# Moving 640 columns of the first w1 load behind phi, onto DMA engines 0 to 4

## The chip, the cores and the metric

One core of one Trainium2 chip. The metric is the device time of one execution in microseconds (us), on the core that runs it; lower is better.

## The reference, cut to what matters

Sliding-window attention over 8 batches and 8 heads, then a soft mixture of experts over the 4608 tokens:

```python
x = attention(q, k, v).reshape(4608, 512)
logits = x @ phi                       # 32 slots, 4 for each of 8 experts
d = softmax(logits, axis=0); slot_input = d.T @ x
h = maximum(slot_input[e] @ w1[e], 0)  # w1: 8 x 512 x 1024, float32
slot_out[e] = h @ w2[e]                # w2: 8 x 1024 x 512, float32
out = softmax(logits, axis=1) @ slot_out
```

All of w1 and w2 (33.5 MB as float32) is needed once, and only when attention is done. So the weights stream in beside the attention, and the output goes out at the end.

## The kernel before: the parts that matter

The program is a list of operations with reads and writes; a small scheduler in the file orders them for each engine and derives the waits. Two kinds of loads compete. GpSimd issues the software transfers (queue q0), which cast float32 to bf16 on the way: all of q, k, v, w2 and nearly all of w1. SyncE issues the hardware transfers (queue q1), which in this kernel don't cast. One of those is the first thing of the kernel: the first 2048 of the 4096 columns of expert 0's w1, as float32, into space that a w2 load fills much later; ScalarE casts it.

```python
op(SP, lambda: spq.dma_start(
    af(w2off(0), [[1, 2048]]),
    w1_rows(0)[:, :2048]), .1, -200.0,
   kind="dma", nbytes=1 << 20, sem=sem("s_w1f"), writes=b_w2[0], name="w1f")
for x in range(2):
    op(ACT, lambda x=x: act.activation(
        a(o_w1 + 1024 * x, [[1, 1024]]), af(w2off(0) + 2048 * x, [[1, 1024]]), ACTF.Copy),
        1.1, -200.0, reads=b_w2[0], writes=[b_w1[0]], name=f"w1c{x}")
# ... (cut)
def load_phi(first):          # SyncE, after the first transpose of VectorE, about 11.8 us
    op(SP, lambda: spq.dma_start(f(o_phst, [[64, 2], [1, 64]]),
        moe_phi.rearrange("(hf p two) s -> p hf (two s)", hf=2, two=2)), .1, 20.0,
       kind="dma", nbytes=65536, sem=sem("s_phi"), writes=[b_phst], name="phi", after=[first])
```

The order on q0 is: the first batch's k, q, v (six loads), the rest of expert 0's w1, the second batch's loads, and so on, and last of all small slices of w2, after whose landing only 1.3 us of work stand ahead of the next output evictions (ScalarE and VectorE copying finished results to where the stores take them from).

The softmax here doesn't subtract the row's maximum and nothing guards it: scores larger than these inputs give would overflow.

## Time and profile before

| | before |
|---|---|
| time, median | 176.98 us (176.91 to 177.19, 6 runs) |
| span of the profiled run | 175.2 us |
| first packet of q0 | 4.77 us |
| first load of k, completions of its sixteen engines | 6.49 to 7.02 us |
| last weight transfer, completions of its sixteen engines | 148.69 to 151.54 us |

The prediction shows the slices, the queues and the chain of waits. The timeline of the first 6 us (start, duration, engine, line, operation, what ended the idle time) shows the head: SyncE issues the w1 load at 0.74, GpSimd its first k load at 1.23, and ScalarE waits 3.65 us for the w1 rows.

```profile
0.74 0.37 SPq L408 DMA_DIRECT2D ar<-in_moe_w_dram  x1
...
1.23 0.67 POOL L343 DMA_DIRECT2D ar<-in_k_dram  x1 [0.79 <-POOLq L1041]
...
5.67 2.00 ACT L413 ACTIVATE ar<-ar 128x1024 bf16<-128x1024 f32 x2 [3.65 <-DMA ar<-in_moe_w_dram]
```

And the table of stretches (busy time of each engine, then granted clock, DMA share, GB/s) shows the hand-over from q1 to q0: the w1 load moves 434 GB/s between 4 and 5 us, then q0's bf16 writes count half of what they read.

```profile
3.00:4.00 1.00, 0.00 (x0) 0.00 (x0) 0.87 (x1) 0.00 (x0) 1.00 (x3) 1.00 0.82 344
4.00:5.00 1.00, 0.00 (x0) 0.00 (x0) 1.00 (x6) 0.00 (x0) 1.00 (x3) 1.00 1.08 434
5.00:6.00 1.00, 0.00 (x0) 0.00 (x0) 0.56 (x3) 0.33 (x1) 1.00 (x5) 1.00 1.06 200
```

### The profile page before, as it was taken

The page shows a single profiled execution, that of the slowest core. Times are in us where ns is not written, and L with a number is a line of the kernel's source. Part 1 is how long each engine was busy: PE and PEld are TensorE (multiplying, and loading weights), DVE is VectorE, ACT ScalarE, POOL GpSimd, SP SyncE. Part 2 cuts the span into 40 slices and gives each one's busy share as a digit, 9 for nine tenths or more (in the row PEclk, how much of TensorE's full clock was granted, in tenths as well). Part 3 has the DMA queues.
Part 4 walks back from the last instruction along what each step waited for, and adds up shares of the span by engine and source line. Part 5 has one row for each costly group of instructions (what it writes and reads, how often), then busy time and mean ns, then how long its engine had stood idle before and what let it go on. Part 6 is the DMA issues. An engine that isn't in the chain of part 4 may idle for free.

```text
span 175.2 us, 4785 instructions
## 1 busy us (share of the span) xinstructions
PE 127.4 (73%) x2102; PEld 86.0 (49%) x2102; DVE 120.7 (69%) x220; ACT 105.1 (60%) x165; POOL 44.5 (25%) x90
## 2 busy tenths in 40 slices
PE   0008667969998998998988997999776766898000
PEld 0005535746766866776756766776343323442000
DVE  6899497978998998998698798349430002699300
ACT  2404763797978969969868968965603001599000
POOL 7659502406234053027200014940000000000000
PEclk9999995699999999999999999999999999999655
DMA  6999999999999999999999999999999999999997
GB/s 191 228 210 217 211 214 208 219 210 213 216 211 214 217 213 207 218 211 217 213 209 216 217 213 221 215 219 211 209 223 215 210 192 189 270 343 418 449 423 299
DMA packets 14388, 41.26 MB, mean 236 GB/s; under 512 B 1696, under 2 KB 7328, under 8 KB 12064
## 3 DMA queue, kind: packets, MB, share of 16 engines
q0 software_dynamic: 10512, 30.41, 88.3%
q1 hardware_dynamic: 3856, 10.55, 15.7%
q8 instruction: 16, 0.26, 0.5%
q14 instruction: 4, 0.03, 0.0%
HBM read 61.93 MB, written 9.44 MB: 407 GB/s over the span
## 4 chain that ended last, share of the span: by engine, by line
DMA 33%; DVE 24%; PE 22%; ACT 7%; POOL 5%; issue 3%; POOLq 0%; DVEq 0%
DMA ar<-in_moe_w_dram 21%; DMA ar<-in_v_dram 12%; PE ps L529 6%; DVE ar L497 6%; DVE ar L945 6%; ACT ar L568 4%; POOL ar L381 3%; DVE ar L503 3%; PE ps L590 2%; PE ps L713 2%; PE ps L536 2%; DVE ar L634 2%; PE ps L623 2%; PE ps L546 2%; DVE ar L454 2%
## 5 line engine op out<-in xcount | busy, mean ns | idle before, releaser
L568 ACT ACTIVATE ar<-ps 128x1152 bf16<-128x1152 f32 (+1 forms) x32 | 37.9, 1186 | 21.5 <-PE ps L553 10.9
L529 PE MATMUL ps<-ar 128*128 128x320 bf16 (+1 forms) x128 | 23.2, 306 | 16.1 <-DVE ar L503 13.8
L497 DVE STREAM_TRANSPOSE ar<-ar 128x576 uint32<-128x576 uint32 x28 | 32.8, 1237 | 0.6 <-DMA ar<-in_v_dram 0.6
L634 DVE TENSOR_TENSOR ar<-ps,fs 96x768 bf16<-96x768 f32 (+1 forms) x32 | 26.3, 822 | 1.1
L596 ACT ACTIVATE ar<-ps 128x768 bf16<-128x768 bf16 x32 | 24.8, 809 | 3.6 <-PE ps L590 3.1
L529 PEld LDWEIGHTS ps<-ar 128*128 128x128 bf16 x128 | 10.8, 100 | 20.9 <-POOL ar L427 13.7
L623 PE MATMUL ps<-ar 128*128 128x65 bf16 x320 | 15.2, 195 | 3.4 <-ACT ar L568 2.1
L590 PE MATMUL ps<-ar 128*128 128x128 bf16 x192 | 15.8, 229 | 2.4 <-DVE ar L634 2.1
L503 DVE STREAM_TRANSPOSE ar<-ar 128x576 uint32<-128x576 uint32 x12 | 14.6, 1241 | 1.8 <-DMA ar<-in_q_dram 1.8
L623 PEld LDWEIGHTS ps<-ar 128*128 128x128 bf16 x320 | 12.1, 98 | 6.7 <-ACT ar L568 2.9
L345 POOL DMA_DIRECT2D ar<-in_k_dram x14 | 7.5, 541 | 30.5 <-DVE ar L497 15.6
L942 ACT ACTIVATE ar<-ps,fs 128x512 f32<-128x512 f32 (+1 forms) x23 | 11.4, 636 | 5.7 <-PE ps L934 5.7
L590 PEld LDWEIGHTS ps<-ar 128*128 128x128 bf16 x192 | 12.7, 118 | 3.7 <-DVE ar L634 2.3
L630 DVE RECIPROCAL fs<-ps 96x12 f32<-96x12 f32 (+1 forms) x32 | 6.5, 203 | 10.9 <-PE ps L623 10.6
L885 PE MATMUL ps<-ar 128*32 128x512 bf16 (+1 forms) x76 | 10.8, 347 | 4.3 <-DMA ar<-in_moe_w_dram 3.3
L945 DVE TENSOR_SCALAR ar<-ps,fs 128x512 f32<-128x512 f32 (+1 forms) x23 | 12.7, 627 | 1.0 <-PE ps L934 1.0
L934 PE MATMUL ps<-ar 128*128 128x512 bf16 (+1 forms) x46 | 10.2, 346 | 1.1 <-DVE ar L909 1.0
L343 POOL DMA_DIRECT2D ar<-in_q_dram x16 | 8.8, 549 | 6.1 <-DVE ar L509 6.1
L713 PE MATMUL ps<-ar 128*128 128x288 bf16 x64 | 9.8, 299 | 0.7 <-ACT ar L697 0.7
L693 ACT ACTIVATE ar<-ps 128x1024 bf16<-128x1024 bf16 x8 | 8.2, 1030 | 3.3 <-PE ps L680 3.3
L690 ACT ACTIVATE ar<-ps 128x576 bf16<-128x576 bf16 x16 | 9.5, 648 | 1.1 <-PE ps L674 0.8
L509 DVE STREAM_TRANSPOSE ar<-ar 128x160 uint32<-128x160 uint32 (+1 forms) x32 | 9.6, 413 | 0.0
(78 smaller groups left out, 190.2 us busy)
## 6 DMA issues: line engine op xcount, KB each, us to landing
ar<-in_moe_w_dram POOLq DMA_DIRECT2D x13, 1024.0 KB, 26.6
ar<-in_k_dram POOLq DMA_DIRECT2D x16, 288.0 KB, 14.5
ar<-in_q_dram POOLq DMA_DIRECT2D x16, 288.0 KB, 16.2
ar<-in_v_dram POOLq DMA_DIRECT2D x16, 288.0 KB, 15.2
out_dram<-ar SPq DMA_DIRECT2D x2, 2048.0 KB, 10.1
out_dram<-ar SPq DMA_DIRECT2D x10, 256.0 KB, 3.1
out_dram<-ar SPq DMA_DIRECT2D x2, 1024.0 KB, 6.1
ar<-in_moe_w_dram SPq DMA_DIRECT2D x1, 1024.0 KB, 4.9
```

What stands on the lines that cost most here:

```text
L497: return dve.transpose(au(o_kqv[kq] + 2304 * j + 36 * x, [[1, 18], [36, 16], [576, 2]]), au(src + 64 * 18 * x, [[32, 18], [1, 32]]))
L503: return dve.transpose(au(dst, [[1, 18], [18, 32]]), au(src, [[32, 18], [1, 32]]))
L529: pe.matmul(pf(h, 0, [[1, W]]), a(o_id, [[1, 128]]), a(msk, [[1, W]]), start=True, stop=False)
L568: eo = op(ACT, lambda P=P, W=W: act.activation(a(P, [[W, 4], [1, W]]), AP(ps, 0, [[4096, 128], [512, 4], [1, W]]), ACTF.Exp, scale=SCALE), ...
L590: last = pe.transpose(pb(bank.idx, bb * 256 + par * 32, [[64, 4], [1, 32]]), src, a(o_id, [[1, 128]]))
L596: op(ACT, lambda t=t, bank=bank: act.activation(a(o_vb[vs] + 3 * t * VBK, [[66, 12], [2, 32], [1, 2]]), pb(bank.idx, 0, [[64, 12], [1, 32] ...
L623: last = pe.matmul(pf(bank.idx + x, 65 * t, [[1, 65]]), w, a(VB + t * VBK + 66 * h, [[1, 65]]), start=True, stop=True)
L634: op(DVE, lambda hp=hp, bank=bank: dve.tensor_tensor(a(ox + 128 * hp, [[64, 2], [256, NT], [1, 64]], 0, rows), pf(bank.idx, 0, [[512, 2], ...
L713: last = pe.matmul(pf(bank.idx, 0, [[1, 288]]), a(o_phis + 128 * c, [[1, 128]]), a(o_xt[xt] + 576 * c + 288 * g, [[1, 288]]), start=(c == ...
L885: last = pe.matmul(pf(sobank[x].idx, 0, [[1, n]], 32 * j, 32), a(o_htz + 1024 * g + 128 * c + 32 * j, [[1, 32]]), a(w2off(e) + DM * c + co ...
L942: op(ACT, lambda: act.activation(dst, src(), ACTF.Copy, scale=sca), actt(cw, .1), prio + .1, reads=[bank, b_rinv], writes=wr, name=f"OE{G} ...
L945: op(DVE, lambda: dve.tensor_scalar(dst, src(), sca, None, op0=AluOp.mult), dvet(cw, True) + .08, prio + .1, reads=[bank, b_rinv], writes= ...
```

## The change

The intent: some DMA engines finish their share of the loads 2.4 us before the others. The first load is shortened for all sixteen, and what is taken away is given to engines 0 to 4 alone, later. ScalarE casts the first 1408 columns, GpSimd the other 640.

```diff
-    op(SP, ... w1_rows(0)[:, :2048] ... name="w1f")
-    for x in range(2):
-        op(ACT, ... 1024 columns ...)
+    WX = 1408
+    def w1_first(n, c0, c1, p0, pn, **kw):
+        op(SP, lambda: spq.dma_start(af(w2off(0) + 2 * c0, [[1, c1 - c0]], p0, pn),
+                                     w1_rows(0)[p0:p0 + pn, c0:c1]), .1, ...)
+    def w1_cast(n, c0, c1, prio):
+        ... op(POOL if n else ACT, lambda: pool.tensor_copy(dst, src) if n else act.activation(dst, src, ACTF.Copy), ...)
+    w1_first(0, 0, WX, 0, 128, prio=-200.0)
+    w1_cast(0, 0, WX, -200.0)
+    def w1_rest(first):
+        w1_first(1, WX, 2048, 0, 125, prio=21.0, after=[first], lag=8.0)
+        w1_first(2, WX, 2048, 125, 3, prio=22.0, after=[first], lag=8.0)
+        w1_cast(1, WX, 2048, 30.0)
...
             load_phi(first_t[0])
+            w1_rest(first_t[0])
```

(Waits and buffers of the helper are cut.)

More of the change, by code (lines that the diff above doesn't have):

```diff
@@ L405, in load_w @@
                    writes=list(wr) + rd + ([x for y in b_kqv[0] for x in y] if name[:2] == "w2" and e in (3, 4) else []))
-    op(SP, lambda: spq.dma_start(
-        af(w2off(0), [[1, 2048]]),
-        w1_rows(0)[:, :2048]), .1, -200.0,
-       kind="dma", nbytes=1 << 20, sem=sem("s_w1f"), writes=b_w2[0], name="w1f")
-    for x in range(2):
-        op(ACT, lambda x=x: act.activation(
-            a(o_w1 + 1024 * x, [[1, 1024]]), af(w2off(0) + 2048 * x, [[1, 1024]]), ACTF.Copy),
-            1.1, -200.0, reads=b_w2[0], writes=[b_w1[0]], name=f"w1c{x}")
+    WX = 1408
+    b_w1f = [Buf("w1fa"), Buf("w1fb")]
+    def w1_first(n, c0, c1, p0, pn, **kw):
+        op(SP, lambda: spq.dma_start(af(w2off(0) + 2 * c0, [[1, c1 - c0]], p0, pn),
+                                     w1_rows(0)[p0:p0 + pn, c0:c1]), .1,
+           kind="dma", nbytes=1024 if n else 1 << 20, sem=sem(f"s_w1f{n}"), writes=[b_w1f[n > 0]] + b_w2[0],
+           name=f"w1f{n}", **kw)
+    def w1_cast(n, c0, c1, prio):
+        dst, src = a(o_w1 + c0, [[1, c1 - c0]]), af(w2off(0) + 2 * c0, [[1, c1 - c0]])
+        o = op(POOL if n else ACT, lambda: pool.tensor_copy(dst, src) if n else act.activation(dst, src, ACTF.Copy),
+            actt(c1 - c0), prio, reads=[b_w1f[n]], writes=[b_w1[0]], name=f"w1c{n}")
+        for x in b_w2[0]:
+            x.r.append(o)
+    w1_first(0, 0, WX, 0, 128, prio=-200.0)
[4 more added lines that the diff above has]
+        w1_cast(1, WX, 2048, 30.0)
     def const_ops():
```

## The prediction

> **What bounds the kernel now.** I read three views in this order. First the page's forty slices and its queue table. A slice is 4.38 us of the 175.2 us span.
>
> ```profile
> DVE  6899497978998998998698798349430002699300
> ...
> DMA  6999999999999999999999999999999999999997
> GB/s 191 228 210 217 211 214 208 219 210 213 216 211 214 217 213 207 218 211 217 213 209 216 217 213 221 215 219 211 209 223 215 210 192 189 270 343 418 449 423 299
> ...
> q0 software_dynamic: 10512, 30.41, 88.3%
> q1 hardware_dynamic: 3856, 10.55, 15.7%
> q8 instruction: 16, 0.26, 0.5%
> ```
>
> The DMA row has a nine in every slice but the first and the last. The loads run on q0, are cast from float32 to bf16 on the way, and fill the engines' time until about 151 us; then q1 stores the output until the end. No compute engine is near that: VectorE is the busiest of them in the first two thirds and idles after it.
>
> Second, the chain of waits that ended last, from 108 us on.
>
> ```profile
> 109.37 4.05 POOL ar L381 x6
> ...
> 115.33 36.21 DMA ar<-in_moe_w_dram
> 151.54 0.04 issue
> 151.58 0.30 PE ps L885
> 151.88 0.02 issue
> 151.90 0.44 DVE ar L909
> 152.34 0.05 issue
> 152.39 0.42 PE ps L934 x2
> 152.81 0.03 issue
> 152.84 8.63 DVE ar L945 x15
> ```
>
> The last weight transfer is issued at 115.33 us and lands at 151.54 us. Its 36.21 us are queueing, since it is only 64 KB: GpSimd issues far ahead of the transfers, so a delay of a few us in an issue costs nothing. From the landing it is about 1.3 us to the next evictions, and then 21 us of stores. The kernel therefore ends when **the slowest of the sixteen DMA engines** has moved its share.
>
> Third, the engines are not equally late. The page can't show that, but the trace keeps, for each transfer, the sixteen moments at which its semaphore is counted up, one for each engine. For the last weight transfer seven engines finish at 148.69 to 149.21 us, one at 149.77, and eight at 151.05 to 151.54. For the first load of k all sixteen lie between 6.49 and 7.02 us. So eight engines fall 2.4 us behind on the way. The sixteen instruction fetches on q8 account for it: 0.5% of sixteen engines' 175.2 us is 14 us, or 0.9 us for each fetch of 16 KB, and two of them on each of eight engines give the lag, with some waiting. The table of stretches agrees: the engines' share falls just when seven of them are out of loads and the stores have not begun.
>
> ```profile
> 148.00:149.00 1.00, 0.71 (x7) 0.71 (x8) 0.49 (x2) 0.37 (x1) 0.00 (x0) 1.00 1.23 163
> 149.00:150.00 1.00, 0.97 (x10) 0.63 (x7) 1.00 (x4) 1.00 (x4) 0.00 (x0) 1.00 0.77 103
> 150.00:151.00 1.00, 0.93 (x8) 0.42 (x6) 0.79 (x3) 0.56 (x2) 0.00 (x0) 1.00 1.14 241
> ```
>
> The last two columns are the share of the DMA engines (above 1 where packets overlap) and the GB/s: 0.77 and 103 between 149 and 150 us.
>
> **What the Trainium skill says.** "DMA: Bandwidth & Descriptors", section "Why a DMA increments its semaphore by 16 and not by 1", says that a transfer runs on the largest number of engines up to 16 that divides its slowest dimension, and that hardware transfers take the lowest-numbered ones. 125 partitions give 5 engines, 25 rows each, and 3 partitions give 3 engines, one row each. That is the point of the odd split. Every hardware transfer of the kernel before uses all sixteen, so its trace neither confirms nor denies this. Section "Queues, rings and completion order" says that an engine goes round-robin between queues, switching at whole packets. The trace fits it at the start: q0's first packet starts at 4.768 us, 6 ns after the first engine has finished its share of the first w1 load, and not before. Section "Latency and other measured facts" puts the first byte of a software transfer at about 1 us. GpSimd's first load is issued at 1.23 us and takes 0.67 us, so by that it is ready near 2.9 us (an estimate from that page) and has been waiting behind w1; no record shows when it was ready. "GPSIMD Engine Reference", section 4.1, says that one-input elementwise work on GpSimd is roughly at line rate; no such cast is in the trace before.
>
> **The change part by part.**
>
> Taken from the start: the first w1 load shrinks from 2048 to 1408 float32 columns, so its rows from 8192 to 5632 bytes, eight rows to an engine. The trace has 309 ns for an undisturbed 8192-byte packet of that load and 22 ns for a 256-byte packet of phi. A straight line through the two is 13 ns plus 0.036 ns a byte: 217 ns for 5632 bytes and 105 ns for 2560 bytes (estimates). Each engine saves 8 x (309 - 217) = 0.74 us, and q0 starts at about 4.0 us in place of 4.77, if it is ready by then, which the 2.9 us above says it is.
>
> Added behind phi, from about 12 us on: 25 x 105 = 2.63 us on engines 0 to 4, and one row more, 2.73 us, on engines 0 to 2. Net, **engines 5 to 15 have 0.74 us less to do, engines 3 and 4 have 1.89 us more, engines 0 to 2 have 1.99 us more.** The bytes read from memory stay the same.
>
> At the end of the loads: the late eight engines, if none of 0 to 4 is among them, finish at 150.3 to 150.8 us. The early ones that got the extra rows finish at 148.7 to 149.2 plus 2.0, which is 150.7 to 151.2. So the last landing moves from 151.54 to between 150.8 and 151.2, **0.35 to 0.74 us earlier**. The extra of 2 us nearly fills the lag of 2.4 us, which looks like a size chosen for it.
>
> ScalarE's two casts of 1024 columns (1.05 us each, at 5.67 us) become one of 1408, some 1.4 us. ScalarE then idles until 15.53 us: nothing gained. GpSimd gets one cast of 640 columns, which I put at 0.5 to 1 us; GpSimd is 25% busy, and its issues lead the landings by 14 to 26 us (median of the issue table), so nothing lost. SyncE's two issues at 0.38 us each lie beside other work. Earlier landings of the first q, k and v load buy nothing directly: VectorE is at its memsets until 10.57 us and k had landed at 7.02.
>
> From the last landing everything follows at the same distance: the late engines save 0.74 us of their own work, and the chain of PE, VectorE and store follows the landing. Sum: 177.02 - 0.5 = **176.5 us**.
>
> **The rivals.**
>
> One: **engines 0 to 4 are among the late eight.** The records carry no engine numbers, so the trace before can't exclude it. Then their last landing goes from 151.5 to 153.5 and the time to about 179. Against it speaks that the size fits the lag of the other engines so well; I give it one chance in eight.
>
> Two: **q0 is not ready at 4.0 us.** Then the start leaves a hole in place of a gain, the late engines end where they did, and engines 0 to 2 end at 148.7 to 149.2 plus 2.7, up to 151.9: between no change and 0.3 us slower, so 177.0 to 177.3. The fit of the first-byte figure speaks against it.
>
> Three: **GpSimd's queue stalls.** Its cast stands in program order among the load issues, and waits for rows that alternate with q0's packets (362 ns for 4608 bytes): up to 26 x (105 + 362) = 12 us after phi's first packet at 15.54, so until 27.7 us. Loads behind it would be issued late. The 14 us or more that an issue leads its landing cover that, except where the next batch's q, k, v land late and VectorE waits. Its wait for loads of v is only 0.6 us in all now, and batch 1's two k loads land at 18.3 and 19.7 us for a use at 23.23: 3.5 us of slack against at most 2 us of delay. The end would hardly see it.
>
> Four: **the time is hidden by the stores.** Engines out of step at 151 us have come into step at 155.3 to 155.7 us for the sixth store (the same completion records), because it waits for evictions. If evictions rather than the engines set the pace there, only the landing of the last weights counts, and the gain is the lower figure, 0.35 us. That stays within the range.
>
> **Range and chances.** The main line gives 176.3 to 176.7, rivals two and four 176.7 to 177.3, run to run spread is 0.3 us. An 8 in 10 range of 175.9 to 177.4 leaves out rival one. Two per cent is 3.5 us. More than the 0.74 us cannot be saved, so faster by over 2% is nearly excluded (0.01). Even rival one gives only 1%, so slower by over 2% needs it together with a stall (0.03).
>
> **What would show it.** Right: q0's first packets near 4.0 us; new q1 packets of 2560 bytes, 128 of them, near 105 ns; the sixteen completions of the last weight transfer within about 1 us, the last at 150.8 to 151.2; a higher share of the DMA engines between 149 and 150 us; the chain of waits still through the last weight transfer. Wrong: a first q0 packet still at 4.77 (rival two); a last landing after 152 us with a few engines alone at the end (rival one); a long wait of GpSimd's new cast followed by VectorE waiting for loads (rival three).

## The result, and the profile after

The changed kernel takes 177.61 us (177.53 to 177.77, 6 runs) against 176.98. The ratio is 1.0034 with a 95% interval of 1.0022 to 1.0047: within 2%, but clearly slower, where 0.5 us faster was predicted. Ratios here are the mean time of one kernel's fast runs over that of the other's of the same rounds, so not quite the ratio of the quoted medians.

The page of the changed kernel, slices and queues:

```profile
DMA  6999999999999999999999999999999999999997
GB/s 169 194 212 232 227 216 215 216 214 207 221 213 208 220 212 207 220 211 210 219 212 208 218 218 213 222 214 216 213 216 218 204 197 184 263 343 418 451 421 298
DMA packets 14524, 41.26 MB, mean 235 GB/s; under 512 B 1704, under 2 KB 7336, under 8 KB 12328
## 3 DMA queue, kind: packets, MB, share of 16 engines
q0 software_dynamic: 10512, 30.41, 88.2%
q1 hardware_dynamic: 3992, 10.55, 15.8%
q8 instruction: 16, 0.26, 0.5%
```

The same bytes, 128 more data packets on q1, and an unchanged picture: the engines are as full as before. The GB/s of the first two slices fell (169 and 194 from 191 and 228), and the fourth and fifth, in which the moved rows travel, hold more (232 and 227 from 217 and 211). Nothing here says why it is slower.

The chain of waits does. Its columns are start, length and what ran or was waited for. From the last issue on it has the same pieces as before, with the landing at 152.08 in place of 151.54:

```profile
115.39 36.70 DMA ar<-in_moe_w_dram
152.08 0.04 issue
152.13 0.29 PE ps L903
152.42 0.02 issue
152.45 0.44 DVE ar L927
152.89 0.05 issue
152.93 0.42 PE ps L952 x2
153.36 0.03 issue
153.38 8.64 DVE ar L963 x15
```

The issue is 0.06 us later, the landing 0.54 us, the time of the profiled run 0.56 us. So the loss is in the queueing of the DMA engines, and GpSimd's cast isn't it: the timeline of the changed kernel has that cast at 28.03 us, 0.73 us long and with no wait ahead of it.

```profile
5.03 1.38 ACT L419 ACTIVATE ar<-ar 128x1408 bf16<-128x1408 f32 x1 [3.01 <-DMA ar<-in_moe_w_dram]
...
12.29 0.72 SPq L412 DMA_DIRECT2D ar<-in_moe_w_dram  x2
...
28.03 0.73 POOL L419 CAST ar<-ar 128x640 bf16<-128x640 f32 x1
```

Which engines are late? The sixteen completion times of one transfer, out of the trace's semaphore records, sorted (they carry no engine numbers):

```
first load of k
  before   6.49 6.59 6.60 6.63 6.64 6.66 6.68 6.77 6.83 6.92 6.93 6.96 6.97 6.98 7.01 7.02
  changed  5.87 5.97 5.97 6.05 6.06 6.08 6.12 6.12 6.15 6.19 6.20 6.33 6.40 6.52 6.68 7.55
a load of q, about 31 us
  before   31.52 31.63 31.67 31.68 31.69 31.82 31.86 32.00 32.07 32.08 32.10 32.11 32.15 32.17 33.36 33.47
  changed  31.09 31.23 31.29 31.30 31.33 31.43 31.70 31.71 31.83 32.45 32.69 33.84 33.93 33.97 34.11 34.28
last weight transfer
  before   148.69 148.87 148.91 148.93 149.03 149.17 149.21 149.77 151.05 151.26 151.34 151.36 151.38 151.42 151.43 151.54
  changed  148.34 148.49 148.77 150.31 150.57 150.59 150.60 150.66 150.90 151.03 151.07 151.16 151.30 151.65 151.93 152.08
```

Three things are to be seen. At the start most engines are 0.6 to 0.7 us early, but one is late: 7.55 us, where the latest had been 7.02. At 31 us five engines stand apart at 33.84 to 34.28, on average 2.59 us behind the first nine of the row, which have neither fetched instructions yet nor got extra rows. I take those five for engines 0 to 4: the semaphore of the transfer of 125 rows has one record half a us after its issue and then five, at 22.92 to 24.14 us, and that of the 3 rows one and then three; five engines carried the one and three the other, though no record numbers them. At the end three early engines are left of eight, so all five came out of the early eight. The balance that was planned did happen, and it was overdone: the last landing went up, not down.

An engine can be followed all the same, by how far its completion stands behind the earliest one of the same load: from load to load that distance stays within some 0.05 us, unless something holds the engine up. Three loads of the changed kernel, by the time of their earliest completion:

```
 13.09   0.00 0.09 0.12 0.13 0.18 0.19 0.20 0.22 0.23 0.25 0.32 0.44 0.59 0.60 0.69   1.47
 21.35   0.00 0.19 0.21 0.23 0.23 0.24 0.33 0.64 0.64 0.73   1.60   2.80 2.87 2.88 3.27 3.28
148.34   0.00 0.15 0.43   1.97 2.23 2.25 2.27 2.32 2.56 2.69 2.74 2.82 2.96 3.31 3.59 3.75
```

- **The fetching eight.** In the kernel before, after the first of the sixteen instruction fetches (23.56 us) one completion stands apart, after the second two, and so on up to eight. From the ninth fetch on, one after another falls back a second time. Each step is 1.0 to 1.2 us.
- **The straggler of the start** isn't one of the five. At 21.35 us, before any fetch, it stands alone at 1.60 us, and the five at 2.80 to 3.28; with both faults it would be near 4. (So it is the 32.69 of the row above; the 32.45 has had one fetch.) It falls back at the fifth and the thirteenth fetch and ends at 151.93 us.
- **The last one**, at 152.08 us, is one of the five. It falls back by another 0.54 us between the loads that begin to land at 103.74 and 108.57 us. The eighth early engine of the kernel before (149.77 us) does the same, by 0.52 us, between 108.92 and 113.79 us, and stands with the other seven until then. What holds it there stays open.

So two faults reach the end within 0.15 us of each other: in this run either of them alone would have kept the last landing at 151.9 us or later.

The table of stretches agrees. The dip of the DMA share, in which engines wait for the first stores, is still there and came later (0.77 between 149 and 150 us before):

```profile
148.00:149.00 1.00, 0.32 (x3) 0.15 (x3) 0.43 (x1) 0.00 (x0) 0.00 (x0) 1.00 1.24 167
149.00:150.00 1.00, 1.00 (x10) 0.93 (x10) 0.61 (x2) 0.72 (x2) 0.00 (x0) 1.00 1.16 155
150.00:151.00 1.00, 0.97 (x10) 0.58 (x9) 1.00 (x4) 1.00 (x4) 0.00 (x0) 1.00 0.78 114
```

### The profile page after: what moved, and what is told of

Same layout as the page of the kernel before. It is cut to its first block, busy times and chain, and to the rows that moved or that the text cites. A ratio compares the mean times of both kernels' runs of the same rounds, so it can differ in the third digit from the quotient of the medians.

```text
span 175.8 us, 4788 instructions
## 1 busy us (share of the span) xinstructions
PE 126.6 (72%) x2102; PEld 85.2 (48%) x2102; DVE 120.8 (69%) x220; ACT 104.6 (60%) x164; POOL 45.3 (26%) x91
## 4 chain that ended last, share of the span: by engine, by line
DMA 45%; DVE 25%; PE 10%; POOL 5%; ACT 4%; issue 3%; POOLq 0%; DVEq 0%
DMA ar<-in_v_dram 24%; DMA ar<-in_moe_w_dram 21%; DVE ar L514 8%; DVE ar L963 6%; PE ps L546 3%; POOL ar L381 3%; DVE ar L520 3%; PE ps L607 2%; ACT ar L585 2%; DVE ar L471 2%; DVE ar L651 2%; POOL ar L345 1%; DVE ar L476 1%; PE ps L553 1%; DVE fs L780 1%
## 5 line engine op out<-in xcount | busy, mean ns | idle before, releaser
L903 PE MATMUL ps<-ar 128*32 128x512 bf16 (+1 forms) x76 | 11.6, 379 | 3.9 <-DMA ar<-in_moe_w_dram 3.1
L903 PEld LDWEIGHTS ps<-ar 128*32 128x32 bf16 x76 | 4.7, 101 | 10.7 <-DMA ar<-in_moe_w_dram 6.4
L730 PE MATMUL ps<-ar 128*128 128x288 bf16 x64 | 9.2, 287 | 0.9 <-ACT ar L714 0.9
```

Source lines behind the costliest of these rows:

```text
L903: last = pe.matmul(pf(sobank[x].idx, 0, [[1, n]], 32 * j, 32), a(o_htz + 1024 * g + 128 * c + 32 * j, [[1, 32]]), a(w2off(e) + DM * c + co ...
```

## The experiments

**Theory.** The time is the last weight landing plus a constant; the landing is that of the latest of sixteen engines. Two things made the latest later: one of engines 0 to 4 had been 0.6 us behind the other early ones already (149.77 against 149.21), so that 2 us more put it past the old end; and an early start of q0 leaves one to three engines with a stall that eats their gain. **Rivals.** GpSimd's cast or the compute engines are behind it; or only one of the two is.

First the constant, from all profiles in which the compute work kept its place. "k late" is the last completion of the first load of k less the median one.

| kernel | first q0 packet | longest q0 packet before 6 us | k late | last weight landing | time of that run | difference |
|---|---|---|---|---|---|---|
| before | 4.77 | 0.22 | 0.22 | 151.54 | 176.99 | 25.45 |
| changed | 3.98 | 1.55 | 1.42 | 152.08 | 177.55 | 25.47 |
| e1_all16 | 3.81 | 1.60 | 1.57 | 152.96 | 178.45 | 25.49 |
| e2_head_only | 3.99 | 1.95 | 1.62 | 151.72 | 177.17 | 25.45 |
| e3_tail_only | 4.78 | 0.20 | 0.48 | 152.39 | 177.92 | 25.53 |
| e4_seven | 4.01 | 1.48 | 1.19 | 152.38 | 177.83 | 25.45 |
| e5_half | 4.46 | 0.42 | 0.22 | 151.22 | 176.73 | 25.51 |
| e7_k_touched | 4.34 | 0.54 | 0.74 | 152.61 | 178.08 | 25.47 |
| e9_second_384 | 4.70 | 0.29 | 0.27 | 151.38 | 176.88 | 25.50 |
| e10_second_640 | 4.81 | 0.20 | 0.25 | 151.83 | 177.34 | 25.51 |
| e11_touch_1152 | 4.00 | 1.12 | 1.00 | 152.83 | 178.28 | 25.45 |
| e12_1152 | 3.56 | 0.94 | 2.42 | 153.69 | 179.19 | 25.50 |
| e13_1792 | 4.42 | 0.40 | 0.61 | 151.23 | 176.73 | 25.50 |

Over a range of 2.5 us of landings the difference stays within 0.08 us. So each experiment can be read at one number, the last landing. (e6_dve_quiet, e8_pool_quiet and e14_no_head delay the compute work or the stores as well, and have 28.4, 27.8 and 36.7 us.)

### e1_all16: the same columns behind phi, over all sixteen engines

```diff
-        w1_first(1, WX, 2048, 0, 125, ...)
-        w1_first(2, WX, 2048, 125, 3, ...)
+        w1_first(1, WX, 2048, 0, 128, ...)
```

> The changed kernel, but the 640 columns behind phi go as one transfer of 128 partitions over all sixteen engines. Theory (the latest engine at the last weight landing sets the time, and engines 0 to 4 were overfilled because one of them was 0.6 us late already): every engine loses 8 x 111 ns = 0.89 us and gains about 0.5 us at the start, so the last weight transfer lands near 151.9 us in place of 151.54 and the time is about 177.4; seven engines and an eighth stay 2 us early at the end. Rival (splitting the first w1 load is harmful by itself, by a stall at the start or by GpSimd's cast): the same 177.6 as the changed kernel, with a straggler at the start. Rival (only the placement costs): back to 177.0.

Measured: 177.88 us (177.46 to 178.45), ratio 1.0036 (1.0019 to 1.0052). The profiled run was the slowest of the four, with three engines late on the first k load (7.12, 7.33 and 7.74 us against a median of 6.17) and the last landing at 152.96. So with no engine favoured the loss is as large: putting rows on engines 0 to 4 can't be all of it. The theory's 151.9 us and 177.4 us were too low; the rival with a straggler at the start comes nearer. The spread of 1 us between runs is new as well, against 0.3 us for the kernel before.

### e2_head_only: the short first load alone

The 640 columns aren't loaded; the cast takes loaded columns twice. Its output is wrong, which doesn't matter for the time.

```diff
-        w1_first(1, WX, 2048, 0, 125, ...)
-        w1_first(2, WX, 2048, 125, 3, ...)
-        ... src = af(w2off(0) + 2 * c0, ...), reads=[b_w1f[n]]
+        ... src = af(w2off(0) + 2 * (c0 - (1408 if n else 0)), ...), reads=[b_w1f[0]]
```

> The first load shrunk to 1408 columns, and the other 640 columns not loaded at all (the cast takes loaded columns again, so the result is wrong on purpose). Theory: this shows what the start saves: about 0.5 us on most engines, last landing near 151.0, time about 176.5, and a straggler at the start, if it is a regular thing, can take it back. Rival (the start saves the 0.74 us of the prediction): last landing 150.8, time 176.2. Rival (the start saves nothing): 177.0.

Measured: 176.95 us (176.72 to 177.32) against 177.16, ratio 0.9993 (0.9976 to 1.0010): no measurable gain, though 0.33 MB less is loaded. The chain of this kernel:

```profile
114.64 37.08 DMA ar<-in_moe_w_dram
151.72 0.04 issue
151.76 0.30 PE ps L902
```

The sixteen completions of the last weight transfer tell why: 148.19 148.43 148.49 148.54 148.57 148.80 149.75 150.30 150.64 150.65 150.78 150.79 150.86 150.90 151.06 151.72. Rank by rank thirteen are 0.4 to 0.6 us earlier than in the kernel before, two in the middle are 0.5 us later, and the last is 0.18 us later. The first load of k shows two stragglers: completions at 5.91 to 6.46, then 7.31 and 7.78. Followed from load to load, one of these falls back at the fourth and the twelfth fetch and is the last one of the end, 151.72; the other doesn't fetch and ends at 150.30, where it does no harm. Two packets of q0 that start at 4.23 and 4.33 us take 1.50 and 1.95 us; of 2304 bytes written, they take 0.19 us elsewhere. **The head part gains half a microsecond on most engines and nothing on the one that counts.**

### e3_tail_only: the extra rows alone

The first load stays whole, and the 640 columns are loaded a second time on engines 0 to 4.

```diff
-    w1_first(0, 0, WX, 0, 128, prio=-200.0)
-    w1_cast(0, 0, WX, -200.0)
+    w1_first(0, 0, 2048, 0, 128, prio=-200.0)
+    w1_cast(0, 0, 1024, -200.0)
+    w1_cast(0, 1024, 2048, -200.0)
```

> The first load whole, as before, and the 640 columns loaded a second time behind phi on engines 0 to 4 (the cast repeats the same values). Theory: engines 0 to 4 get 2.8 to 3.0 us more; the one of them that was at 149.77 lands at about 152.6, the others of them at 151.5 to 152.2; the fetching eight stay at 151.05 to 151.54; time about 178.0. Rival (all five engines of 0 to 4 were among the seven early ones): last landing 152.1, time 177.6. Rival (0 to 4 are among the fetching eight): last landing 154.3, time near 179.7.

Measured: 177.92 us (177.92 to 178.13), ratio 1.0049 (1.0034 to 1.0064). The last landing is 152.39 us: between the 152.6 of the theory and the 152.1 of the first rival, far from the 154.3 of the second. So engines 0 to 4 aren't among the fetching eight, and the tail alone costs 0.85 us of landing. No packet of q0 before 6 us is over 0.20 us: with the whole first load there is no stall.

### e4_seven: engines 0 to 6

```diff
-        w1_first(1, WX, 2048, 0, 125, ...)
-        w1_first(2, WX, 2048, 125, 3, ...)
+        w1_first(1, WX, 2048, 0, 119, ...)
+        w1_first(2, WX, 2048, 119, 7, ...)
+        w1_first(3, WX, 2048, 126, 2, ...)
```

> The changed kernel, but the 640 columns go as transfers of 119, 7 and 2 partitions, so over engines 0 to 6 with 18 or 19 rows each in place of 25 or 26. Theory, if engines 5 and 6 fetch no instructions either: the late one of 0 to 4 lands near 151.3, the fetching eight at 150.5 to 151.0 (a straggler apart), time 176.7 to 176.9. If engine 5 or 6 is a fetching one: it lands near 153 and the time is about 178.4.

Measured: 178.48 us (177.83 to 179.45), ratio 1.0082 (1.0040 to 1.0124). The profiled run, the fastest of the four, lands last at 152.33 and 152.38 us, and three engines stay early (148.20 to 148.61), as many as with engines 0 to 4 alone. If 5 and 6 were early ones, one would be left. So this points to 5 and 6 being fetching engines, and to five being the right number. Followed from load to load, two of the seven that got rows do fall back at a fetch, at the seventh and eighth (69.51 and 75.72 us) and again at the fifteenth and sixteenth, and end last. That they are engines 5 and 6 is an inference, as no record names an engine.

### e5_half: 320 columns

```diff
-    WX = 1408
+    WX = 1728
```

> The changed kernel with 1728 columns in the first load and 320 behind phi on engines 0 to 4. The runs so far show that with a first load of 1408 columns one to three engines spend 1.3 to 1.9 us on a q0 packet that starts near 4.3 us, and that with 2048 columns none does. Theory S (the stall depends on how early q0 starts): q0 starts near 4.4 us, the stall is half as long or gone, the last landing is near 151.1 us and the time 176.7. Rival (the stall is of fixed length once q0 starts before GpSimd has issued its seven loads): a packet of 1.3 us or more again, last landing 151.8, time 177.2.

Measured: 176.77 us (176.73 to 176.83) against 176.94, ratio 0.9986 (0.9971 to 1.0001). q0 starts at 4.46 us, no packet is over 0.42 us, k's completions lie between 6.35 and 6.73, all earlier than before. The chain:

```profile
114.80 36.41 DMA ar<-in_moe_w_dram
151.22 0.04 issue
151.26 0.30 PE ps L903
```

With half the amount, both faults are gone and the sign turns, by 0.32 us of landing; the interval of the time just touches 1.

### e6_dve_quiet, e7_k_touched, e8_pool_quiet: what stalls the first packets?

```diff
# e6: VectorE's memsets at the start wait for ScalarE's first cast
+        if eng == DVE: kw["after"] = list(kw.get("after", ())) + [cast0]
# e7: one transfer of k ahead of the first w1 load
+    op(SP, lambda: spq.dma_start(f(o_phst, [[1, 64]]), k[0, 0:4]...[:, 0:64]), .1, -201.0, ...)
# e8: GpSimd's third load waits for the first w1 load
+            dma_in(fn, ..., after=[head] if b == 0 and (j, x) == (2, 0) else [], ...)
```

> The changed kernel with VectorE's memsets held back until ScalarE has cast the first columns, so VectorE is idle while q0 starts. Only the first 10 us are looked at; later everything is some 5 us late and the time says nothing. If VectorE's writes stall the first q0 packets: no packet of q0 before 8 us over 0.6 us. If not: one to three of 1.3 us or more near 4.3 us, as in the changed kernel.

> The changed kernel with one more transfer ahead of the first w1 load: 128 rows of 256 bytes of k, on all sixteen engines, into space that phi fills later. If the stall is the first touch of k by an engine, it is taken here: no q0 packet over 0.6 us, first completions of k within 0.6 us of each other, last landing about 0.2 us after that of an unstalled start, time 177.3 (engines 0 to 4 still overfilled). If the stall is of another kind: packets of 1.3 us again, time 177.6 to 177.8.

> The changed kernel, but GpSimd issues only the first two loads at once and waits for the first w1 load to land (about 5 us) before the third. If GpSimd's issuing while q0 starts causes the stall: no q0 packet over 0.6 us near 4.3 us. If not: packets of 1.3 us or more there again. The time may be a little longer if q0 runs dry near 6.8 us.

e6: with VectorE idle until 7.2 us, three packets of q0 still take 1.14 to 1.45 us, and two engines finish the first k load at 7.20 and 7.21 us. VectorE isn't the cause.

e8: GpSimd's issues stop at 2.4 us, and a packet from 3.73 to 5.01 us is there nevertheless (1.28 us). "k late" was only 0.74 us, so issuing may add to the stall, but it isn't needed for it. The run itself went astray: GpSimd did its other start work first and issued the third load at 10.82 us, the queue ran dry, and the time is 185.66 us.

e7: no packet over 0.54 us, but the added transfer also moved q0's start to 4.34 us, where e5_half has no stall either. Its completions of k still lie 0.93 us apart. It tells nothing by itself, and at 178.04 us (ratio 1.0058, 1.0041 to 1.0075) it costs more than the change.

### e9_second_384 and e10_second_640: rebalancing without an early start

The first load stays whole. The columns are taken from expert 1's software transfer instead, 384 or 640 of them, and loaded behind phi on engines 0 to 4.

```diff
-            return pool.dma_start(a(o_w1 + e * 4096 + 1024 * r0, ...), w1_rows(e)[:, 1024 * r0:])
+            return pool.dma_start(a(o_w1 + e * 4096 + s0, ...), w1_rows(e)[:, s0:])   # s0 = MC for e == 1
-        w1_first(1, WX, 2048, 0, 125, ...)     # and the transfer of 3 rows likewise
+        w1_first(1, 0, MC, 0, 125, ...)        # of w1_rows(1), cast to expert 1's place
```

> The first w1 load whole, as before, so q0 starts at 4.77 us and nothing stalls. Instead, 384 columns of the second expert's w1 are taken from its software transfer and loaded behind phi on engines 0 to 4, then cast by GpSimd. Theory (rebalancing pays if no engine's start stalls and the late one of 0 to 4 isn't overfilled): every engine saves about 0.46 us, engines 0 to 4 get about 1.7 us; the last landing is 151.1 to 151.2 us in place of 151.54, time 176.6. Rival (rebalancing itself does not carry over to the end): 177.0.

> The same with 640 columns, the amount of the change, without its early start of q0. Theory: no stall; the fetching eight land at about 150.8 us, but the late one of 0 to 4 at 149.8 + 2.5 (what the tail alone cost) - 0.76, so 151.5 to 151.6; time about 177.0: without the stall the change would still have gained nothing. Rival (the stall alone spoilt the change): last landing 150.9 to 151.2, time 176.5.

e10: 177.42 us against 177.07, ratio 1.0024 (1.0011 to 1.0037). This is the clearest picture of the balance. No packet stalls (0.20 us at most), k is 0.25 us apart, and the last weight transfer's completions fall into three groups: three at 147.87 to 148.19, eight at 150.34 to 150.64, five at 151.14, 151.19, 151.22, 151.52 and 151.83. The eight gained 0.7 to 0.9 us, about the 0.74 us that the prediction wanted; the five, engines 0 to 4, are now the end, 0.2 to 0.3 us later than expected. Its chain:

```profile
114.01 37.11 DMA ar<-in_moe_w_dram
151.12 0.04 issue
151.17 0.67 PE ps L906 x3
151.84 0.04 issue
151.88 0.30 PE ps L906
```

So **without the stall the change would still not have gained**: the five are 1.2 us beyond the eight at their latest. (This chain names an earlier transfer for 151.12 us, as the wait for the last one, at 151.83, is short.)

e9: 176.83 us against 177.07, ratio 0.9990 (0.9977 to 1.0004), last landing 151.38. The landing is 0.16 us earlier than in the kernel before, 0.2 us short of what was expected, and the time's interval includes no change.

### e11_touch_1152 and e12_1152: the stall again

```diff
-    WX = 1408
+    WX = 1152      # e12; e11 the same with e7's transfer of k ahead
```

> The first w1 load at 1152 columns behind a transfer of 128 rows of 256 bytes of k on all engines; q0 should start near 4.0 us, as in the changed kernel. Only the start is looked at. If the stall is each engine's first touch of k: no q0 packet over 0.6 us. If not: one to three of 1.2 us or more.

> The first w1 load at 1152 columns without that transfer; q0 should start near 3.6 us. If the stall depends on how early q0 starts: more or longer stalls than in the changed kernel, ends again at 5 to 6.3 us. Rival (fixed length, a matter of chance): the same one to three packets of 1.2 to 1.9 us. Engines 0 to 4 get 896 columns, so the last landing is near 153 us or later.

e11: q0 starts at 4.00 us as in the changed kernel, every engine has read k before, and still two engines end the first k load at 6.91 and 6.93 us, 1.00 us after the median, one of them with a packet of 1.12 us. So the first touch of k isn't the whole cause. e12: q0 starts at 3.56 us, the median engine ends the k load at 5.54, and two end at 7.83 and 7.96. The last landing is 153.69. Neither expectation fits the packets: none before 6 us is over 0.94 us, so an engine can also be late by several slow packets. Starting q0 earlier made the typical engine earlier and the last one later.

### e13_1792 and e14_no_head: the two that were still open

```diff
-    WX = 1408
+    WX = 1792                                   # e13
# e14: no first load; all 2048 columns behind phi
-    w1_first(0, 0, WX, 0, 128, prio=-200.0)
-    w1_cast(0, 0, WX, -200.0)
+        w1_first(1, 0, 2048, 0, 128, ...)
```

> The changed kernel with 1792 columns first and 256 behind phi on engines 0 to 4. The nine profiles so far have a time of 25.45 to 25.53 us after the last weight landing. With 1728 columns the landing was 151.22 us. Theory: q0 starts near 4.5 us, no stall that matters, the fetching eight land at about 151.2, the late one of 0 to 4 at about 151.1; landing 151.2, time 176.7, clear of the kernel before by a little. If it isn't under 176.9, the half version's small gain was chance.

> No first w1 load at all: all 2048 columns behind phi on all sixteen engines, one cast. q0 has nothing ahead of it, so this shows when each engine can start the first load of k. In every run so far the last engine finished that load at 6.7 to 8.0 us, however early the others did. If single engines can't get k before about 5 to 6 us whatever lies ahead: the first k load again ends at 6.7 us or later on its last engine, though most engines end near 5. If the stall comes from the two queues meeting: all sixteen end by about 5.2 us.

e13: median 176.74 us against 176.96, landing 151.23 as expected; but one of its six runs took 177.84, and the ratio is 0.9997 (0.9976 to 1.0019). So the smaller versions (256, 320, 384 columns) have medians 0.2 us below the kernel before, and none is shown to beat it.

e14: with nothing ahead of it q0 starts at 2.61 us, its longest packet before 6 us is 0.60 us, and all sixteen engines have the first k load by 4.52 to 5.49 us. So single engines are not bound to be late until 6.7 us, as I had thought possible; the stall needs the w1 load ahead, or at least grows with it. Some unevenness (0.82 us after the median) is there even so. **What makes the stall stays open**: it is there when q0 takes over from the w1 load at 4.0 us or earlier, it isn't when q0 takes over at 4.4 us or later ("k late" of 0.61 us in e13 at most), and it isn't VectorE. (The time of 189.28 us is of another kind, with the w1 load missing from the start.)

## Why the prediction was wrong

- **What bounds the kernel: right.** The constant of 25.45 to 25.53 us between the last landing and the end, over thirteen kernels, is stronger than what the prediction argued from one chain. (Its "no compute engine is near that" was misread, without effect: TensorE was busy for 28.58 of the 30 us from 60 to 90 us, more than VectorE's 26.77.)
- **Eight engines fall back, and not 0 to 4: right.** Rival one (0 to 4 among the late eight) is refuted by e3_tail_only: 152.39 us in place of 154.3. That the fetches delay the eight was argued from sizes; the trace shows it in time, with one engine falling back at each of the sixteen, though no run takes the fetches away.
- **The cost of the extra rows: right.** 2.63 to 2.73 us predicted, 2.59 us measured at 31 us. A packet of 2560 bytes took 111 ns on average, against 105 predicted.
- **"Each engine saves ... 0.74 us": wrong for the engine that counts.** q0 did start at 3.98 us, and 5632 bytes did take 215 ns. But the saving is 0.4 to 0.6 us on thirteen ranks of sixteen, and one to three packets of q0 take 1.1 to 1.95 us in every kernel with 1408 columns first but e7_k_touched, whose q0 starts later. e2_head_only shows the sum: nothing gained (0.9993), because a stalled engine that also fetches ends last, at 151.72. The prediction named a hole at the start as rival two, but made it a matter of when q0 is ready as a whole; q0 was ready, and single engines were not.
- **"The early ones that got the extra rows finish at 148.7 to 149.2 plus 2.0": this step failed too.** It counts seven early engines. There are eight that don't fall back, and the eighth stood at 149.77 in the prediction's own first paragraph. Five of the eight got the extra rows, and with 0.5 us saved and 2.6 added the eighth would land at 151.9; the five end at 151.83 in e10_second_640 although the eight there have the full saving, and the changed kernel's last landing is 152.08. By the prediction's own net of 1.9 to 2.0 us the eighth would have stood at 151.7 to 151.8: no gain at all. That the late one of 0 to 4 is the former eighth is not shown by an engine number; the sum fits it within 0.2 us, and in both kernels it is an engine without fetches that falls back by 0.5 us at about the same time.
- **GpSimd (rival three): no stall of its queue by the cast**, which takes 0.73 us with no wait. **The stores (rival four)**: they don't hide the landing, time follows it one for one.
- **The range.** It leaned on "more than 0.74 can't be saved" and had 0.4 us above the old time, from rival two. With the eighth engine and the smaller saving counted, a landing of 151.9 and a time of 177.4 would have been the middle and not the end of it; the 0.2 us from there to the measured 152.08 are not accounted for. The sign that the prediction gave for rival one, a last landing after 152 us, came true by another cause.

The Trainium skill, as the prediction used it: that 125 rows go to five engines ("DMA: Bandwidth & Descriptors", "Why a DMA increments its semaphore by 16 and not by 1") agrees with the five completions of that transfer and the five engines that stand apart at 31 us; that they are the lowest-numbered no record shows. The switching at whole packets, which the prediction found to fit the start, fits it only if an engine's eight rows count as one packet: e14_no_head shows that q0 can start at 2.61 us, and in the kernel before it starts at 4.77, when the first engine's eight rows are done. That one-input work on GpSimd is near line rate ("GPSIMD Engine Reference", section 4.1) agrees: 640 columns in 0.73 us, where ScalarE took 1.38 us for 1408.

## What to carry to other kernels

When a kernel ends with a stream of transfers, the latest of the sixteen engines can set its end, as in all thirteen kernels of the table: look at the sixteen completions of the last load, not at the mean busy share, and plan with each rank of that list, the worst included. A rebalancing that fits the lag exactly has no room for one engine that is already behind; here half the amount turned a loss of 0.6 us into a median 0.2 us below the kernel before, which isn't shown to be a gain. And a saving at the start of a queue counts only if every engine gets it: compare the last engine, not the typical one.

## What the Trainium skill lacked or had wrong

- No page says how instruction fetches of 16 KB (sixteen here, 0.94 us each on average) fall on the sixteen DMA engines, or what that costs the loads there. Here eight engines take two each, and at each fetch one engine falls 1.0 to 1.2 us behind; at the end the eight stand 2.4 us behind the others.
- "DMA: Bandwidth & Descriptors" gives a first byte of software transfers at about 1 us (section "Latency and other measured facts"). e14_no_head agrees for the first engine: its packet starts at 2.61 us, 0.71 us after GpSimd's issue of 1.23 to 1.90 us ends. What it lacks is that single engines can lag far behind the first: with a w1 load of 1408 columns ahead and q0 starting by 4.02 us, one to three of the first packets took 1.1 to 1.95 us, and with 2048 columns none was over 0.29 us.
- The same page, section "Bandwidth", tabulates whole transfers on sixteen engines and has no table of measured times of single rows on one engine: here 22, 111, 215 and 309 ns for rows of 256, 2560, 5632 and 8192 bytes (phi's, the moved rows' and the first w1 load's packets; 256 and 2560 are means, the other two undisturbed).
